# A new order of the pieces, block 1 normalized with ScalarE's negated mean, and two weight loads cut differently

## Chip, cores and metric

The kernel runs on one NeuronCore of a Trainium2 chip. The metric is the device time of one execution in microseconds (us). Below, PE is TensorE, DVE is VectorE, ACT is ScalarE, POOL is GpSimd, and SP is the engine that issues most of the transfers (DMAs).

## The reference

The input is normalized per row. Two branches read the result, and both are added to the input: an attention in which every position looks at itself and at seven earlier positions, two apart, with 32 heads of 20 elements, and a feed-forward layer with a GELU.

```python
# S, D, F, H = 2048, 640, 1536, 32
def _A_ref(x, wqkv, wo):
    Dh = D // H
    W, dil = 8, 2
    qkv = (x @ wqkv).reshape(B, S, 3, H, Dh).transpose(2, 0, 3, 1, 4)
    q, k, v = qkv[0], qkv[1], qkv[2]
    idx = jnp.arange(S)[:, None] - (jnp.arange(W) * dil)[None, :]
    mask = idx >= 0
    ...
    logits = jnp.einsum("bhsd,bhswd->bhsw", q, kg) * Dh ** -0.5
    logits = jnp.where(mask[None, None, :, :], logits, -1e9)
    attn = _softmax(logits, axis=-1)
    o = jnp.einsum("bhsw,bhswd->bhsd", attn, vg)
    return o.transpose(0, 2, 1, 3).reshape(B, S, D) @ wo

def _B_ref(x, w1, b1, w2, b2):
    return jnp.einsum("bsf,fd->bsd", _gelu(jnp.einsum("bsd,df->bsf", x, w1) + b1), w2) + b2

xn = _layernorm(x, axis=-1)
return x + _A_ref(xn, A_wqkv, A_wo) + _B_ref(xn, B_w1, B_b1, B_w2, B_b2)
```

## The kernel before

The 2048 rows are cut into four chunks n = 0 to 3 of 512 rows, and each chunk into four blocks of 128 rows. All products on TensorE work on transposed data: features (or heads) lie on the 128 partitions, rows lie along the free dimension.

The kernel is written as 627 small functions with names, the pieces, and a list `ORDER` (L40) of these names. The last lines run the pieces in this order, and each engine executes its instructions in the order in which they were recorded. The waits between engines are put in by the framework, from which instruction writes or reads which part of a tile, and from what was recorded before. So the list sets all queues at once. A name is made of a kind and of numbers, the first of which is the chunk:

- `st`, `su`, `ng`, `sq`, `rs`, `rc`, `xn`: mean, variance, their reciprocal root, and the normalized rows. In chunks 0 and 1 VectorE finds the statistics (`st`, L210); in chunks 2 and 3, and in block 1 of chunk 0, ScalarE does it: sum (`su`, there `sum1`), negated mean (`ng`, there `neg1`), squares (`sq`). `mean1` (L240) turns ScalarE's sum for block 1 into a mean on VectorE. `xn` of chunk 0 is on VectorE (L263), of the others on ScalarE.
- `tp`, `tc`: the transposition, in chunk 0 by TensorE and a copy, in the others by a DMA from SP (L294).
- `ga`, `gb`, `gd`, `ge`, `gc`, `hj`, `hc`: chunk 0's projections to q, k and v in half width, and ScalarE's evictions. `pj` and `pc` are the same for the other chunks: `pj110` is chunk 1, k (0 is q, 1 is k, 2 is v), tile 0. One `pj` is five matmuls of 512 columns into one result bank of the pool `psA`, which has four; `pc` empties it.
- `pad` (L404): ScalarE copies the last 14 columns of the chunk before to the front of a chunk's k or v, since the window looks back 14 positions. `pad11` is the copy for chunk 1's k.
- `qk` (L430): VectorE multiplies a block of q with the eight shifted windows of k; `pa`, `pb` add tiles, `lg` sums over a head's elements with TensorE into the tile `L`.
- `cp`, `mask`, `m`, `mx`, `ex`, `ss`, `ri`, `at`: the softmax, in chunk 0 in two halves a and b. `ri` is a logarithm and an exponential on ScalarE, so it needs another table of ScalarE than the GELU.
- `xe`, `av`, `ac`, `ad`, `ot`: the weights are spread over the partitions by DMA, multiplied with v and summed.
- `f1`, `ge` (`f10_7` is chunk 0, tile 7): the first feed-forward product (five matmuls into a bank of `psA`) and the GELU that empties it.
- `t`, `u`, `ut`, `ud`: second feed-forward product and output projection into two other banks, eviction with bias, turning back by DMA, and a DMA that adds to the output, where `xp` has put x before. The last chunk's `o` pieces make rows directly, and `dh`, `dl`, `dd` add x and store.
- `ldx`, `ld2`, `ldo`: loads of the later x, of the second feed-forward weights and of the output weights, on SP in the order of the list. The first loads stand ahead of the list.

The list before has, around chunk 0's softmax (dots for pieces left out):

```python
hj201 su23 pb04 ... sq22 pj104 pad11 pc103 lg0 ... mx0a mx0b pj120 qk10 ex0a ...
sq21 qk11 ... ss0b ... ss0a ri0b ... qk13 rs2 hc212 ri0a ... rc2 qk12 f10_8 ge0_4 ge0_7
```

Of the kernel before, what the change touches and what calls it, by code (L numbers as in the profile page):

```python
# [11 lines left out]
ALU = mybir.AluOpType  # L12
# [4 lines left out]
S, D, F, H, W, DIL = 2048, 640, 1536, 32, 8, 2  # L17
# [3 lines left out]
KT, FT = D // P, F // P  # L21
# [16 lines left out]
COLS = ((0, 2), (2, 4), (4, 5))  # L38

ORDER = """  # L40
pad01 pad02 st00a st00 sum1 rs00 neg1 xn00a sq1 xn00b tp00a wa tp00b tc00a wb ga tc00b rs01 mean1 gb2 xn01a gb3 xn01b
tp01a st03a tp01b gb4 tc01a tc01b st02a gd gc0 st02 ge st03 rs02 hj101 xn02 rs03 gc4 xn03 gc1 tp02 st13a tp03 st11a
hj100 tc03 st10a st10 tc02 hj102 st13 hc101 hj012 hc100 st12a hj112 st12 hc102 tb hj111 st11 b1 ho rs1 hj110 hc112 rc1
qk00 hc012 pk xn11 hj011 xn10 tc11 hj200 hc111 hc110 tc10 qk01 hj010 hc011 hc200 f10_11 xn13 hc010 tc13 f10_0 xn12
qk03 f10_3 tc12 f10_1 ge0_11 ldx ge0_0 qk02 f10_5 ge0_1 pj110 ge0_5 ld2 pj114 pc110 pa00 su20 pj102 ge0_3 pj100 pc102
pa01 su22 pj112 pc100 su21 f10_2 pb01 pc114 pj103 ge0_2 pc112 xp2 hj201 su23 pb04 ldo pj101 hc201 ng2 sq22 pj104 pad11
pc103 lg0 pj111 cp0b cp0a pc101 mask pj113 m0b xp0 pc104 m0a pc111 xp1 hj211 pc113 mx0a mx0b pj120 qk10 ex0a pj122
pc120 ex0b t040 sq21 qk11 pj124 pc122 hc211 hj210 sq23 t000 sq20 ss0b hj212 hc210 f10_7 ss0a ri0b pc124 pj121 qk13 rs2
hc212 ri0a f10_4 pc121 f10_6 rc2 qk12 f10_8 ge0_4 ge0_7 t001 xn21 f11_1 xn20 tc21 at0b ge0_8 pa11 t041 ge0_6 tc20
pj123 f11_10 xn23 pa10 ge1_1 tc23 f11_9 xn22 ge1_10 f10_9 tc22 at0a pc123 pb11 ge1_9 hj202 xe01 su33 t042 xe03 f11_3  # L50
pad21 xe00 su32 pb14 pj210 ge1_3 xe02 pj203 pc210 su31 lg1 hc202 t002 su30 av01 pj204 ng3 ge0_9 pj214 sq32 pc204 pj211
av00 pc203 ac01 pad12 pc214 pj200 sq30 f11_0 pc200 pc211 av02 ac00 f11_5 sq31 cp1a f10_10 cp1b ge1_0 pj213 av03 ge0_10
ge1_5 pj201 pc213 sq33 t003 pj221 m1 t043 mx1 rs3 pj224 pc221 ac03 ex1 pj202 pc201 rc3 ss1 xn31 pj220 pc202 tc31 ac02
f11_6 pc224 ri1 pj223 at1 ad01 xe11 pj222 pc223 xe12 xe13 pj212 ad00 pc222 xn32 f12_3 xe10 pc220 ot00 xn33 f11_2 ot01
tc32 av11 t004 t044 u00 tc33 t010 u04 av12 t011 ut00 xn30 t012 t030 tc30 t013 av13 t014 ud00 t031 u01 ac11 t032 t033
ac12 t020 t034 ge1_6 av10 ge2_3 t021 pc212 t022 f12_4 ac13 ac10 t023 ge2_4 t024 u03 ut01 xb ad11 f12_6 ot11 pj302 qk22
f11_8 pc302 ge1_2 f11_7 pj303 qk23 ge1_7 ge1_8 pj311 ge2_6 pc303 pj300 pa21 t140 pc300 pj310 f11_11 ad10 pj314 ge1_11
ot10 pc311 f11_4 pc310 qk20 pj301 ge1_4 pc314 pj313 u02 pc301 ut02 t130 qk21 pc313 f13_6 pad31 pad22 ut03 t141 ut04
ud01 pj304 pa20 pj312 ud02 t142 pc312 f12_9 pb21 pc304 ud03 ge3_6 f13_4 t143 pb24 f12_2 f13_1 ge2_2 ge2_9 lg2 f12_10
qk31 cp2a ge3_4 t131 cp2b t132 t133 t134 m2 qk30 f13_0 f13_2 ge3_0 ge2_10 t144 u13 mx2 ge3_2 pj321 qk32 u14 ge3_1  # L60
pj322 t100 pa30 t110 ex2 t101 f13_5 qk33 t102 ge3_5 f13_10 pad32 pc321 pc322 t103 t104 ss2 t111 pa31 ri2 f12_0 u10
f13_3 ut10 at2 f13_8 pb31 xe20 t120 xe22 ge3_8 t112 xe21 ge2_0 t113 ge3_3 pb34 f12_8 xe23 t114 lg3 u11 f12_11 cp3a
av20 ut11 ud10 cp3b f13_9 ge2_11 ge3_10 f13_7 ge2_8 m3 ge3_9 f12_5 ac20 ge3_7 mx3 t121 av21 f12_1 ex3 t122 o300 ss3
t123 ac21 ge2_1 f13_11 av23 t124 ri3 o301 u12 f12_7 at3 av22 pj323 xe31 ge2_5 ut12 ud11 ud04 ge2_7 pj324 t200 t201
ac22 xe30 t230 ut13 pj320 ac23 o302 pc320 ad21 pc323 t202 pc324 xe33 t231 ge3_11 ut14 ad20 t232 o310 ot21 t233 ot20
t203 o311 av31 t204 t234 u20 ut20 av30 t210 u23 ud12 t211 xe32 t212 t213 t214 ac30 t220 u21 ac31 t221 t222 t223 ad30
t224 av33 t240 u22 ud13 ud20 ut21 ud14 t241 t242 t243 ac33 o330 o331 t244 o303 u24 ud21 ut22 ot30 o320 av32 o304 ud22
ut23 ut24 o321 ud23 o312 ac32 o313 dh0 dl0 o332 ad31 o322 dd0 o314 ud24 ot31 o323 dl1 o324 dh1 dd1 o333 dl2 o334 dh2
dd2 ohi dl3 dlo dh3 dhi
""".split()  # L70


# [1 line left out]
def kernel(  # L74
# [16 lines left out]
    nc = tc.nc  # L91
# [23 lines left out]
    wqkv = [wts.tile([P, KT, D], BF16, name=f"w{s}_sb") for s in "qkv"]  # L115
# [5 lines left out]
    wqkv_v = A_wqkv.rearrange("(t p) n -> p t n", p=P)  # L121
    w1_v = B_w1.rearrange("(t p) n -> p t n", p=P)

    def load_x(b0, b1):
        nc.sync.dma_start(x_sb[:, b0:b1, :], x_nb[:, b0:b1, :])

    def load_w(s):
        nc.sync.dma_start(wqkv[s][:], wqkv_v[:, :, s * D : (s + 1) * D])
# [3 lines left out]
    nc.scalar.dma_start(x_sb[:, 1, :], x_nb[:, 1, :])  # L132
    nc.scalar.dma_start(b_rt[0:FT, :], B_b1.rearrange("(t p) -> t p", p=P))
    nc.scalar.dma_start(b_rt[FT : FT + KT, :], B_b2.rearrange("(t p) -> t p", p=P))
    load_w(0)
    load_x(2, BPC)
    load_w(1)
    load_x(BPC, 2 * BPC)
# [9 lines left out]

    def do_ld2():
        w2_v = B_w2.rearrange("(t p) n -> p t n", p=P)  # L150
        for c in range(4):
            ts = slice(c * FT // 4, (c + 1) * FT // 4)
            nc.sync.dma_start(w2_sb[:, ts, :], w2_v[:, ts, :])

    def do_ldo():
# [11 lines left out]
    def table(name):  # L167
# [6 lines left out]
    mask = consts.tile([H, W, MW], BF16, name="mask")  # L174
    nc.gpsimd.memset(mask[:], 0.0)
    nc.gpsimd.affine_select(
        out=mask[:],
# [16 lines left out]
    mv = consts.tile([P, NCH * BPC, nc.vector.BN_AGGR_DIM], F32, name="mv")  # L194
# [3 lines left out]
    acc = consts.tile([P, NCH * BPC], F32, name="acc")  # L198
    neg = consts.tile([P, NCH * BPC], F32, name="neg")
# [17 lines left out]
    def xn_tile(n, bl):  # L217
        return get(("xn", n, bl), lambda: lnp.tile([P, D], BF16, tag="xn", name="xn"))

    def col(tile_, n, bl):  # L220
        i = n * BPC + bl
        return tile_[:, i : i + 1]
# [14 lines left out]
            accum_out=mv[:, n * BPC + bl, 1:2],  # L237
        )

    def do_mean1():  # L240
        nc.vector.tensor_scalar(
            out=mv[:, 1, 0:1], in0=col(acc, 0, 1), scalar1=1.0 / D, scalar2=None, op0=ALU.mult
        )

    def do_rs(n, b0, b1):
        sl = slice(n * BPC + b0, n * BPC + b1)
        summed = n in ACT_STATS or (n, b0) == (0, 1)
        table(LOG_SET)
        nc.scalar.activation(
            logv[:, sl], mv[:, sl, 1], ACT.Ln, bias=eps_t[:], scale=1.0 / D if summed else 1.0  # L250
        )
        nc.scalar.activation(rstd[:, sl], logv[:, sl], ACT.Exp, scale=-0.5)
# [10 lines left out]
    def do_xn(n, bl, a=0, b=KT):  # L263
        i, cs = n * BPC + bl, slice(a * P, b * P)
        xn = xn_tile(n, bl)
        if n:
            nc.scalar.activation(xn[:], x_sb[:, i, :], ACT.Identity, bias=col(nmr, n, bl), scale=col(rstd, n, bl))
            return
        nc.vector.tensor_scalar(
            out=xn[:, cs],  # L270
            in0=x_sb[:, i, cs],
            scalar1=mv[:, i, 0:1],
            scalar2=rstd[:, i : i + 1],
            op0=ALU.subtract,
            op1=ALU.mult,
        )

# [444 lines left out]
    def piece(name, fn, *args):  # L722
        assert name not in pieces
        pieces[name] = lambda: fn(*args)

    for name in "tb b1 mean1 ho ldx ld2 ldo ohi mask pk xb".split():
        piece(name, locals()[f"do_{name}"])
    for u, a, b, eng in (("a", 0, 2, "ve"), ("b", 2, KT, "se")):
        for bl in range(2):
            piece(f"xn0{bl}{u}", do_xn, 0, bl, a, b)  # L730
            piece(f"tp0{bl}{u}", do_tp, 0, bl, a, b, True)
        piece(f"tc00{u}", do_tc, 0, 0, a, b, "ve")
        piece(f"tc01{u}", do_tc, 0, 1, a, b, eng)
    for bl in range(BPC):
        if bl != 1:
            piece(f"st0{bl}a", do_st, 0, bl, 0)
            piece(f"st0{bl}", do_st, 0, bl, 1)
        piece(f"rs0{bl}", do_rs, 0, bl, bl + 1)
        if bl > 1:
            piece(f"xn0{bl}", do_xn, 0, bl)  # L740
            piece(f"tp0{bl}", do_tp, 0, bl, 0, KT)
            piece(f"tc0{bl}", do_tc, 0, bl, 0, KT, "se")
# [119 lines left out]
```

## Time and profile before

| | |
|---|---|
| median of 3 runs | 206.21 us (205.78 to 206.46) |
| the profiled execution | 205.85 us, its span 203.8 us |
| TensorE busy | 199.1 us, 98% of the span |
| VectorE busy | 186.3 us, 91% |
| ScalarE busy | 128.7 us, 63% |
| DMA | 27.31 MB, mean 134 GB/s |
| GELU evictions `hT<-hps` on ScalarE | 36, 686 ns each |
| evictions `kT<-pps` on ScalarE | 15, 594 ns each |
| ScalarE's table loads | 14, 1283 ns each |
| products `prod<-qT,kT` on VectorE | 16, 2820 ns each |

The span goes from the first to the last instruction that was profiled; the time of an execution has some 2 us around it. An engine's busy time is the union of its instructions. Lines of the view by time give the start in us, the time until the last of the group ended, engine, line of the program, operation, what is written and what is read, sizes, and how many instructions stand in the group; in brackets the idle time of the engine before it and who ended it.

### The profile page before, as it was taken

Reading aid. Unit: us, or ns where it says so; the run is one execution under the profiler, and the core shown is the slowest. Engines: PE = TensorE matmul, PEld = TensorE weight load, DVE = VectorE, ACT = ScalarE, POOL = GpSimd, SP = SyncE. Lnnn points to the kernel's source line nnn. Section 1 sums busy time; section 2 is a strip of 40 time slices with the busy share of each in tenths; the row PEclk is TensorE's granted clock in tenths of the full one; section 3 lists DMA queues with packets and bytes.
Section 4 is the critical chain, followed back from the end, with each engine's and each line's share of the span. In section 5 each row is a group of like instructions: output and inputs, shape, how many; then the busy total and the mean of one; then the engine's idle time right before and its main releaser. Section 6 shows DMA issues by size and latency. Waiting matters only on the chain.

```text
span 203.8 us, 2855 instructions
## 1 busy us (share of the span) xinstructions
PE 199.1 (98%) x1082; PEld 105.7 (52%) x1100; DVE 186.3 (91%) x161; ACT 128.7 (63%) x237; POOL 29.4 (14%) x34
## 2 busy tenths in 40 slices
PE   8999999999999999999999999999999999999994
PEld 3999456564454455444454443444434454444552
DVE  2899999699998999999999997999978999998972
ACT  5679988799899997647264635398669923221000
POOL 2000000000000400004420040000202704046210
PEclk9999999999999999999999999999999999999999
DMA  6996499910246681779896190000496799897851
GB/s 213 388 397 197 120 328 341 400 72 3 64 86 184 112 148 32 164 147 117 144 152 71 37 92 0 3 0 0 92 186 123 126 169 129 97 106 88 77 90 64
DMA packets 38430, 27.31 MB, mean 134 GB/s; under 512 B 25106, under 2 KB 34578, under 8 KB 38418
## 3 DMA queue, kind: packets, MB, share of 16 engines
q1 hardware_dynamic: 28016, 20.39, 37.4%
q0 software_dynamic: 10080, 6.56, 27.2%
q10 hardware_dynamic: 322, 0.20, 0.3%
q8 instruction: 8, 0.13, 0.3%
q14 instruction: 4, 0.03, 0.0%
HBM read 10.49 MB, written 4.59 MB: 74 GB/s over the span
## 4 chain that ended last, share of the span: by engine, by line
PE 96%; ACT 1%; issue 1%; DVE 0%
PE T L701 27%; PE hps L619 25%; PE pps L338 23%; PE gps L382 7%; PE lo L657 5%; PE idle L448 2%; PE both L657 2%; PE gps L351 2%; PE hi L657 1%; PE L L485 1%; ACT x_sb L704 1%; PE tp L284 1%; ACT wq_sb L635 1%; ACT hT L635 0%; DVE prod L669 0%
## 5 line engine op out<-in xcount | busy, mean ns | idle before, releaser
L619 PE MATMUL hps<-xnT,w_sb 128*128 128x512 bf16 x231 | 55.8, 379 | 0.4
L435 DVE TENSOR_TENSOR prod<-qT,kT 128x5120 bf16<-128x5120 bf16 x16 | 44.6, 2820 | 1.2 <-PE L L485 1.0
L701 PE MATMUL T<-hT,w_sb 128*128 128x512 bf16 x179 | 44.0, 379 | 0.1
L619 PEld LDWEIGHTS <-w_sb 128*128 128x128 bf16 x240 | 23.3, 98 | 28.0 <-issue 1.0
L713 POOL DMA_DIRECT2D out_dram<-x_sb x15 | 19.7, 1430 | 84.0 <-DMA x_sb<-x_sb 63.0
L635 ACT ACTIVATE hT<-hps,bT 128x512 bf16<-128x512 f32 x36 | 23.5, 686 | 9.4 <-PE hps L619 9.1
L701 PEld LDWEIGHTS <-w_sb 128*128 128x128 bf16 x180 | 17.4, 98 | 20.5 <-issue 0.4
L704 ACT ACTIVATE x_sb<-T,bT 128x512 bf16<-128x512 f32 x15 | 10.3, 687 | 21.8 <-PE T L701 14.8
L589 DVE TENSOR_TENSOR prod<-vT,ax 128x5120 bf16<-128x5120 bf16 x8 | 22.3, 2821 | 1.8 <-PE L L485 1.8
L589 DVE TENSOR_TENSOR prod<-vT,x_sb 128x5120 bf16<-128x5120 bf16 x8 | 22.3, 2820 | 0.1
L600 POOL DMA_DIRECT2D prod<-prod x6 | 7.8, 1300 | 80.4 <-DVE prod L589 80.4
L170 ACT ACT_TABLE_LOAD x14 | 18.0, 1283 | 1.0 <-PEq L846 0.7
L476 DVE TENSOR_TENSOR prod<-prod 128x4096 bf16<-128x4096 bf16 x8 | 18.3, 2290 | 0.2
L338 PE MATMUL pps<-xnT,wq_sb 128*128 128x512 bf16 x74 | 18.3, 379 | 0.1
L701 PE MATMUL T<-oT,wo 128*128 128x512 bf16 x73 | 18.2, 379 | 0.1
L470 DVE TENSOR_TENSOR prod<-prod 128x4096 bf16<-128x4096 bf16 x8 | 18.1, 2286 | 0.1
L338 PE MATMUL pps<-xnT,wk_sb 128*128 128x512 bf16 x75 | 18.2, 379 | 0.0
L338 PE MATMUL pps<-xnT,wv_sb 128*128 128x512 bf16 x71 | 17.8, 379 | 0.2
L602 DVE TENSOR_TENSOR prod<-prod 128x2560 bf16<-128x2560 bf16 x10 | 14.7, 1488 | 0.1
L338 PEld LDWEIGHTS <-wk_sb 128*128 128x128 bf16 x75 | 8.7, 118 | 7.7 <-issue 0.4
L338 PEld LDWEIGHTS <-wv_sb 128*128 128x128 bf16 x75 | 8.8, 117 | 7.4
L338 PEld LDWEIGHTS <-wq_sb 128*128 128x128 bf16 x75 | 8.8, 117 | 7.3
(96 smaller groups left out, 241.5 us busy)
## 6 DMA issues: line engine op xcount, KB each, us to landing
prod<-prod POOLq DMA_DIRECT2D x6, 640.0 KB, 7.0
ax<-attn SPq DMA_DIRECT2D x8, 256.0 KB, 4.3
x_sb<-attn SPq DMA_DIRECT2D x8, 256.0 KB, 4.8
w_sb<-in_B_w_dram SPq DMA_DIRECT2D x2, 960.0 KB, 11.3
w_sb<-in_B_w_dram SPq DMA_DIRECT2D x4, 480.0 KB, 8.2
out_dram<-x_sb SPq DMA_DIRECT2D x3, 640.0 KB, 9.5
out_dram<-x_sb POOLq DMA_DIRECT2D x15, 128.0 KB, 5.1
x_sb<-in_A_x_dram SPq DMA_DIRECT2D x2, 640.0 KB, 6.9
```

Of the source, the lines that this page charges most:

```text
L170: nc.scalar.preload_act_table_set(name)
L338: nc.tensor.matmul(ps[:], lhsT=wqkv_p[which][:, ti, to, :], rhs=xnT[:, ti, :], start=(ti == 0), stop=(ti == KT - 1),)
L435: nc.vector.tensor_tensor(out=prod[:, j], in0=q[:, :, at].unsqueeze(1).to_broadcast([P, W, KT, P]), in1=window(k, at), op=ALU.mult,)
L470: nc.vector.tensor_tensor(out=low, in0=low, in1=high, op=ALU.add)
L476: nc.vector.tensor_tensor(out=first, in0=first, in1=rows[:, :, t * P : (t + 1) * P], op=ALU.add)
L589: nc.vector.tensor_tensor(out=prod[:, j], in0=window(qkv_tile(n, 2), slice(j * P, (j + 1) * P)), in1=ax_view(n)[:, j, :, :].unsqueeze(2).t ...
L602: nc.vector.tensor_tensor(out=low, in0=low, in1=high, op=ALU.add)
L619: nc.tensor.matmul(ps[:], lhsT=w1_sb[:, ti, ft * P : (ft + 1) * P], rhs=tiles["xnT", n][:, ti, :], start=(ti == 0), stop=(ti == KT - 1),)
L635: nc.scalar.activation(hT, tiles["hps", n, ft][:], ACT.Gelu_apprx_tanh, bias=bT[:, ft : ft + 1], scale=1.0)
L657: nc.tensor.matmul(out_ps(bl, hi), lhsT=lhs, rhs=rhs[:, CH:D] if hi else rhs[:, 0:CH], start=pc == 0 and k == 0, stop=pc == 4 and k == len ...
L701: nc.tensor.matmul(ps[:], lhsT=lhs, rhs=rhs, start=pc == 0 and k == 0, stop=pc == 4 and k == len(srcs) - 1)
L713: nc.gpsimd.dma_start(dst, src, accum_op=ALU.add)
```

## The change

Four things are changed.

- The list of pieces is in another order. It holds the same pieces but `mean1`.
- `mean1` is gone. Block 1 of chunk 0 is normalized by adding ScalarE's negated mean instead of subtracting a mean.
- q's weights are loaded by two DMAs (two and three of the five slices of 128 input features), not by one.
- The second feed-forward weights are loaded by three DMAs of four tiles, not by four of three.

```diff
-    load_w(0)
+    for a, b in ((0, 2), (2, KT)):
+        nc.sync.dma_start(wqkv[0][:, a:b, :], wqkv_v[:, a:b, 0:D])
     load_x(2, BPC)
...
     def do_ld2():
         w2_v = B_w2.rearrange("(t p) n -> p t n", p=P)
-        for c in range(4):
-            ts = slice(c * FT // 4, (c + 1) * FT // 4)
+        for c in range(3):
+            ts = slice(c * FT // 3, (c + 1) * FT // 3)
             nc.sync.dma_start(w2_sb[:, ts, :], w2_v[:, ts, :])
...
-    def do_mean1():
-        nc.vector.tensor_scalar(
-            out=mv[:, 1, 0:1], in0=col(acc, 0, 1), scalar1=1.0 / D, scalar2=None, op0=ALU.mult
-        )
...
             in0=x_sb[:, i, cs],
-            scalar1=mv[:, i, 0:1],
+            scalar1=neg[:, 1:2] if bl == 1 else mv[:, i, 0:1],
             scalar2=rstd[:, i : i + 1],
-            op0=ALU.subtract,
+            op0=ALU.add if bl == 1 else ALU.subtract,
             op1=ALU.mult,
```

The new list, from the first pieces, and around chunk 0's softmax:

```python
pad01 pad02 st00a st00 sum1 ho rs00 neg1 xn00a sq1 xn00b tp00a wa tp00b wb tc00a tc00b rs01 ga xn01a gb2 xn01b tp01a
gb3 st02a tb tp01b tc01a gb4 st02 tc01b gd gc0 st03a ge rs02 st03 hj101 b1 xn02 rs03 gc4 xn03 gc1 tp02 st12a tp03
...
qk02 f10_1 tc12 ge0_0 f10_5 ldx qk03 f10_11 ge0_5 f10_3 ge0_11 ge0_2 pj101 ge0_3 pa00 pj112 pc101 ge0_1 pj104 pc112
xp2 pa01 su20 pj110 xp0 pc104 ld2 su22 pj102 pc110 pb01 pj100 su21 hj201 su23 pc102 pb04 pj103 ng2 pc100 hc201 pj114
sq22 lg0 pc114 ldo pj111 cp0b cp0a sq21 mask pj113 m0b pc103 m0a pj124 pc111 mx0a pc113 mx0b t000 qk11 pj120 ex0b
hj202 ex0a hj210 pc120 sq23 ss0a hj211 pc124 ss0b sq20 pj122 qk13 hc202 rs2 f10_7 pad11 hc211 pc122 t040 ri0b f10_8
ri0a rc2 qk12 hc210 f10_4 f11_1 ge0_7 xn21 qk10 f11_3 ge0_4 tc21 xn20 pj121 ge1_3 tc20 t041 ge1_1 pa11 f11_9 ge0_8
...
```

On the queues of SP and POOL the same kinds of DMAs stand in another order. `xp2` and `xp0` now come ahead of the second feed-forward weights, `xp1` behind the four expansions `xe00` to `xe03`; three of the DMA additions (`ac`) precede the first addition to the output, where two did.

## The prediction

> **What bounds the kernel now.** I read the page's totals, the slices, the chain that ended last, TensorE's waits, and then the order of time on TensorE, ScalarE and VectorE where the two orders differ.
>
> ```profile
> span 203.8 us, 2855 instructions
> PE 199.1 (98%) x1082; PEld 105.7 (52%) x1100; DVE 186.3 (91%) x161; ACT 128.7 (63%) x237; POOL 29.4 (14%) x34
> ...
> PEclk9999999999999999999999999999999999999999
> ...
> PE 96%; ACT 1%; issue 1%; DVE 0%
> ```
>
> TensorE is busy for 98% of the span at full clock, and the chain lies 96% on it. TensorE's list of waits has one line, 0.8 us before the first warm-up matmul. From about 9 us to 200.8 us the matmuls stand almost end to end: 25 matmuls of 512 columns take 5.39 us start to start, 0.2157 us each. So the change can win only what little is not dense. A piece that comes late for TensorE is paid in full, as nothing behind it has slack to absorb it. Hence I looked where the new order makes TensorE wait.
>
> Its result banks (`psA`, four) are emptied by ScalarE in queue order. Around chunk 0's softmax the view by time shows before:
>
> ```profile
> 35.81 0.62 PE L485 MATMUL L<-prod,head_of 128*32 128x512 bf16 x8
> 44.62 0.81 PE L701 MATMUL T<-hT,w_sb 128*128 128x512 bf16 x3
> 45.81 1.24 PE L619 MATMUL hps<-xnT,w_sb 128*128 128x512 bf16 x5
> 47.97 3.40 PE L619 MATMUL hps<-xnT,w_sb 128*128 128x512 bf16 x14
> 51.21 0.81 PE L701 MATMUL T<-hT,w_sb 128*128 128x512 bf16 x3
> ```
> ```profile
> 35.31 0.23 ACT L409 COPY kT<-kT 128x70 bf16<-128x70 bf16 x1
> 37.20 0.58 ACT L525 CAST e<-L 128x512 bf16<-128x512 f32 x1 [1.18 <-DVE e L525]
> 39.76 1.28 ACT L170 ACT_TABLE_LOAD   x1
> 46.63 0.26 ACT L557 ACTIVATE ax<-ax 128x64 f32<-128x64 f32 x1
> 49.27 1.28 ACT L170 ACT_TABLE_LOAD   x1
> 50.57 1.26 ACT L635 ACTIVATE hT<-hps,bT 128x512 bf16<-128x512 f32 x2
> ```
> ```profile
> 36.48 0.69 DVE L525 CAST e<-L 128x512 bf16<-128x512 f32 x1 [0.86 <-PE L L485]
> 40.12 5.56 DVE L435 TENSOR_TENSOR prod<-qT,kT 128x5120 bf16<-128x5120 bf16 x2
> 45.59 0.42 DVE L532 TENSOR_TENSOR ax<-e 128x256 f32<-128x256 bf16 x1
> 46.51 0.42 DVE L532 TENSOR_TENSOR ax<-e 128x256 f32<-128x256 bf16 x1
> 47.44 2.82 DVE L435 TENSOR_TENSOR prod<-qT,kT 128x5120 bf16<-128x5120 bf16 x1
> ```
>
> The reader should see three things. The small copy `pad11` (35.31, L409) starts with no idle time before it, five microseconds ahead of the first product of chunk 1 (40.12). ScalarE is full from 37.2 to 54 us. TensorE meets no gap over that stretch.
>
> **The change part by part.**
>
> *pad11 behind qk11 and qk13.* In the new order `pad11` stands after both products. It writes the first 14 columns of each tile of chunk 1's `kT`; the products read other columns of the same tiles, in interleaved strips. The program built from the changed file has a wait before this copy for the VectorE count that `qk13` reaches. The old one has none. Everything behind `pad11` on ScalarE waits too: `hc211`, `pc122`, both reciprocals, `hc210`, the GELU table, `ge0_7`. TensorE needs the banks that these free.
>
> I lay out both queues from the start of `lg0`, 35.78 (35.81 before; the order ahead of it has the same matmul work). VectorE up to `qk11` is as before, 40.12-35.81 = 4.31 later: 40.09. `qk11` takes 2.74 to the next start (two took 45.59-40.12 = 5.47): 42.83. The two sums now follow at once, 0.92 each (46.51-45.59): 44.67. `qk13` 2.82: done 47.49. Hand-over from VectorE to ScalarE takes 0.03 in this trace (median of six starts): `pad11` starts 47.52.
>
> ScalarE: `cp0a` 37.17, then 0.48 to `sq21`, 0.82 for it, three evictions at 0.477 with 0.17 more before the table load, table 1.29, two exponentials 0.53 each, `pc120` 0.47, `sq23` 0.81, so `pc124` starts 43.71 and is done 44.29. After it come `sq20` 0.81, `hc202` 0.25 and `rs2` 0.5: ScalarE would reach `pad11` at about 45.8. It stands idle 1.7 us there.
>
> TensorE from 35.78: `lg0` 0.55, two k pieces 2.16, `pj124` 1.08, `t000` 0.65, `pj120` 1.08, 25 matmuls of 256 columns 2.72: ready for `pj122` at 44.02. Its four waits, with 0.04 from ScalarE's end to TensorE's start:
> - `pj122` needs `pc124`: 44.33, a stall of 0.3. Then `pj122`, `f10_7` and `t040` (1.08+1.08+0.65) end at 47.14.
> - `f10_8` needs `hc211`: 47.52+0.14 (pad to next, 35.31 to 35.45) = 47.66, +0.59 = 48.25; 48.29, a stall of 1.15.
> - `f11_3`, three pieces later at 51.52, needs `ge0_7`: 47.66 + two evictions 0.95 + two reciprocals 0.90 + `hc210` 0.58 + table 1.29 + GELU 0.69 = 52.07; 52.11, a stall of 0.6.
> - `pj121`, at 53.19, needs `ge0_4`, which stands behind `xn21`: 51.38+0.58+0.81+0.69 = 53.46; 53.50, a stall of 0.3.
>
> Then `f11_9` at about 55.2 finds a bank free at 54.9, and ScalarE is caught up. Sum 2.35. Taken alone, `pj122`'s 0.3 does not come from `pad11`. Without the wait, `f10_8` and `f11_3` find their banks (1.7 earlier) and `pj121` about 0.3 late. So 0.6 belongs to the order and 1.75 to the wait. VectorE loses 0.3, since `qk12` waits for `pad11`; TensorE is then over 2 us later, which more than pays for it.
>
> *Block 1 without `mean1`.* One VectorE instruction less:
>
> ```profile
> 6.48 0.14 DVE L241 TENSOR_SCALAR mv<-acc 128x1 f32<-128x1 f32 x1
> 6.71 0.64 DVE L269 TENSOR_SCALAR xn<-x_sb,mv,rstd 128x256 bf16<-128x256 bf16 x2
> ```
>
> The normalization waits for `rs01` (done 6.50) and could begin up to 0.17 earlier. TensorE has one gap there: two starts 0.154 apart at 8.05 where 0.056 is usual. Gain 0 to 0.1; I take 0.05. `ho` moves ahead of `xn00a` (0.28 of VectorE work); VectorE is idle 0.66 there, so nothing. Without that cover it would delay the first transposes by 0.28.
>
> *q's weights in two parts.* They landed at 5.88 before and were first needed at 6.17. Two of five slices land earlier, the rest must be there when the first ten matmuls are done. One more issue on SP, 0.42, sits ahead of x's blocks 2 and 3, k's weights and all later loads. Blocks 2 and 3 landed 6.99 and were read 7.26; k's weights landed 9.02 and were needed 9.60. Queued bytes, not issues, set these landings (299 GB/s in the first 10 us), so I take 0. At worst 0.42-0.27 = 0.15.
>
> *Second feed-forward weights in three, after `xp2` and `xp0`.* One issue less (0.5). Ahead of the first part now lie two writes of 0.66 MB; at the 400 GB/s that the stretch 36 to 40 us moved, that is 3.3 us, and 31.4 becomes about 35. `t000` reads it at 39.6, so the cover is 4.6 us. `xp1` moves behind the first expansions; x's first rows are overwritten only near 81 us. Both 0.
>
> *The rest of the order* moves evictions by places in their queues. Elsewhere I found each bank emptied at least 0.15 before its reuse. Before had about 0.2 of such gaps itself (two starts 0.40 apart at 57.7), which the new order may lose.
>
> Sum: +2.35 - 0.05 - 0.1 = +2.2. The profiled execution took 205.85 (span 203.8 and 2.05 around it): 208.05. The runs shown have median 206.21, 0.36 above it, so the sum could read 208.4. Since single terms might shrink by overlap, I stay with 208.0.
>
> **The clock.** The granted clock is full in all slices, yet 128-column matmuls start 0.107 apart up to 6.6 us and 0.056 after.
> The Trainium skill ("TensorE: Matmul & The Clock Gate", section "A second HAM failure mode: psum-queue depth-cycling") says that TensorE idling briefly between groups, as banks cycle, can drop its clock again; no run here shows it, as before has no such idling.
>
> **The rivals.**
> 1. *The stall is hidden or absent.* The strips do not truly overlap, so the wait might cost little if `qk13` were earlier, or ScalarE later. For: `pad11` is 0.23 us of work. Against: VectorE is 91% busy and `qk13` cannot start before both sums. Then 0.0 to 0.6 remain: about 206.2.
> 2. *Faster.* The head decides: block 1 earlier, q's weights earlier, and the gaps at 8.05 (0.1), 57.7 (0.2) and around `lg0` (0.2) close, from the point where no bank in 44 to 54 us is late. 205.85-0.5 = 205.35. Against: these are all the gaps there are.
> 3. *The idling takes the clock down.* Price from this trace: the slow stretch at the start lasted from 0.78 to 6.65; half of 5.87 is 2.9 lost. 208.0+2.9 = 210.9. Against: four stalls of which the longest is 1.15. That page of the Trainium skill would have it happen.
> 4. *A transfer comes late too* (x's blocks, or the transposes behind the three moved writes): a further 0.5 to 1, some 208.8.
>
> **How the numbers follow.** Forecast 0.76 (207.3 to 208.7 by itself), rival 1 0.11, rival 2 0.03, rival 3 0.03, rival 4 0.07. About 0.3%, 0.6 us, can be told from no change; against 206.21, faster means below 205.6 and slower above 206.8. Rival 2 gives faster 0.03; rival 1 gives same 0.10 and, with the rest, slower 0.87. The range 206.7 to 209.0 leaves out most of rivals 1 to 3, under 2 in 10.
>
> **What would show it.** After: ScalarE's `kT<-kT` copy starts near 47.5, behind 1.7 us idle released by VectorE's product; TensorE's starts show gaps near 44, 47 to 48 (about 1.1), 52 and 53, and nowhere else over 0.3; the GELU table load comes near 50.1. It is wrong if the copy does not wait, if the gaps sum to under 1, or if gaps appear after 60 us.

## The result, and the profile after

| | before | after |
|---|---|---|
| median | 206.06 us (5 runs, 205.78 to 206.46) | 208.92 us (5 runs, 208.13 to 209.28) |
| profiled execution | 205.85 us, span 203.8 us | 208.92 us, span 206.9 us |
| TensorE busy | 199.1 us | 200.0 us |
| VectorE / ScalarE busy | 186.3 / 128.7 us | 185.8 / 129.0 us |

The ratio is 1.0135, with a 95% interval from 1.0112 to 1.0158: the change costs 2.9 us. In a few executions of the kernels below the granted clock is lower and the time some 2% longer (212.27 us in one of e2_whole_q), and the ratios leave most of these out. The work is the same to within a microsecond on each engine, so the time went into waits. The page of after, from its totals, its slices and its chain:

```profile
span 206.9 us, 2869 instructions
PE 200.0 (97%) x1100; PEld 104.9 (51%) x1100; DVE 185.8 (90%) x160; ACT 129.0 (62%) x237; POOL 29.4 (14%) x34
...
PEclk9999999999999999999999999999999999999999
...
PE 78%; ACT 7%; DVE 7%; DMA 5%; issue 1%
```

The granted clock is full in every slice. The chain, 96% TensorE before, now leaves TensorE for a fifth of the span: there are places where TensorE waits for ScalarE, VectorE and a DMA. TensorE's list of waits in after (line, what it waited for, us in total, times, longest) names them:

```profile
PE hps L615 <- ACT vT L393: 1.0, 1, 1.0
PE hps L615 <- ACT hT L631: 0.8, 2, 0.4
PE idle L444 <- PEq L842: 0.8, 1, 0.8
PE tp L280 <- DVE xn L265: 0.7, 1, 0.7
PE gps L347 <- DVE xn L265: 0.5, 1, 0.5
PE gps L347 <- DVE xnT L285: 0.2, 1, 0.2
```

Before, only the third of these lines was there. The others fall into two places, but for one of the two waits for `hT`, at 24.9, which e3_both below has too at no loss that can be told. The first place is chunk 0's softmax. TensorE, ScalarE and VectorE there, in the view by time of after (start, time until the group's last end, and in brackets the idle time before and who ended it):

```profile
36.91 0.61 PE L481 MATMUL L<-prod,head_of 128*32 128x512 bf16 x8
...
46.52 1.24 PE L615 MATMUL hps<-xnT,w_sb 128*128 128x512 bf16 x5
47.60 0.81 PE L697 MATMUL T<-hT,w_sb 128*128 128x512 bf16 x3
49.44 3.40 PE L615 MATMUL hps<-xnT,w_sb 128*128 128x512 bf16 x15 [1.03 <-ACT vT L393]
53.27 1.24 PE L615 MATMUL hps<-xnT,w_sb 128*128 128x512 bf16 x5 [0.44 <-ACT hT L631]
```
```profile
48.65 0.25 ACT L405 COPY kT<-kT 128x70 bf16<-128x70 bf16 x1 [1.75 <-DVE prod L431]
48.80 0.58 ACT L393 CAST vT<-gps 128x512 bf16<-128x512 f32 x1
...
51.24 1.28 ACT L171 ACT_TABLE_LOAD   x1
52.53 0.69 ACT L631 ACTIVATE hT<-hps,bT 128x512 bf16<-128x512 f32 x1
```
```profile
45.80 2.82 DVE L431 TENSOR_TENSOR prod<-qT,kT 128x5120 bf16<-128x5120 bf16 x1
48.93 5.56 DVE L431 TENSOR_TENSOR prod<-qT,kT 128x5120 bf16<-128x5120 bf16 x2 [0.24 <-ACT kT L405]
```

Read from the copy outwards. The copy `pad11` (48.65, L405) stands behind 1.75 us of idle ScalarE. VectorE's product `qk13`, 45.80 to 48.62, ended that idle time. The eviction of `hc211` starts right behind the copy at 48.80, and TensorE's `f10_8`, which needs the bank, starts at 49.44 after 1.03 us. Start to start, four TensorE gaps above the matmuls' usual pitch lie between 44 and 55 us: 0.21 before `pj122`, 1.19 before `f10_8`, 0.61 before `f11_3`, 0.31 before `pj121`; together 2.32 us.

The second place is the head. `lg0`, the first line of the TensorE fence, starts at 36.91, and before at 35.81: after arrives 1.1 us late at the stretch that the prediction laid out. The head of after on TensorE, from the same view, and then VectorE's first statistics of a block loaded by the later DMA, in after and in before:

```profile
6.07 0.72 PE L347 MATMUL gps<-xnT,wq_sb 128*128 128x128 bf16 x10
7.26 0.47 PE L347 MATMUL gps<-xnT,wq_sb 128*128 128x128 bf16 x5 [0.48 <-DVE xn L265]
...
8.16 0.44 PE L347 MATMUL gps<-xnT,wq_sb 128*128 128x128 bf16 x5
8.81 1.39 PE L347 MATMUL gps<-xnT,wq_sb 128*128 128x128 bf16 x22 [0.21 <-DVE xnT L285]
```
```profile
8.08 0.49 DVE L214 BATCH_NORM_STATS2 stats<-x_sb 128x6 f32<-128x320 bf16 x1 [0.84 <-DMA x_sb<-in_A_x_dram]
7.26 0.49 DVE L213 BATCH_NORM_STATS2 stats<-x_sb 128x6 f32<-128x320 bf16 x1
```

The first ten matmuls of q (`ga`) use the two slices that land first. The eleventh needs the second part and starts 0.7 us after the tenth; it waits for that load's semaphore. The line names VectorE's `xn` as the releaser, but these matmuls do not read it: they read `xnT` of block 0 and q's weights. `xn` of block 1 only happened to end at 7.24. What the matmul waited for, the second part of q's weights, landed at 7.22; a second execution of the same kernel, below, has the DMA's name in this place. Further on, x's blocks 2 and 3 landed at 8.05 (6.99 before), and VectorE waits 0.84 us for them, which it did not before (`st02a`, 7.26 there, no idle time).

1.1 + 2.3 = 3.4 us. Of this some 0.4 comes back by the end: before had a gap of 0.19 near 58 us that after has not, and what follows the last matmul takes 2.8 us in after's span, 3.0 in before's. That leaves 3.0 of the 3.1 us between the two spans.

### The profile page after: what moved, and what is told of

Its sections match the earlier page's. It is cut to its first block, busy times and chain, and to the rows that moved or that the text cites. A ratio compares the mean times of both kernels' runs of the same rounds, so it can differ in the third digit from the quotient of the medians.

```text
span 206.9 us, 2869 instructions
## 1 busy us (share of the span) xinstructions
PE 200.0 (97%) x1100; PEld 104.9 (51%) x1100; DVE 185.8 (90%) x160; ACT 129.0 (62%) x237; POOL 29.4 (14%) x34
## 4 chain that ended last, share of the span: by engine, by line
PE 78%; ACT 7%; DVE 7%; DMA 5%; issue 1%
PE T L697 26%; PE pps L334 21%; PE hps L615 20%; DMA x_sb<-in_A_x_dram 5%; PE lo L653 5%; DVE prod L431 3%; PE both L653 2%; ACT xn L263 2%; DVE stats L214 2%; PE hi L653 1%; ACT L171 1%; PE L L481 1%; ACT hT L631 1%; DVE ax L530 1%; PE gps L378 1%; ACT vT L393 1%
## 5 line engine op out<-in xcount | busy, mean ns | idle before, releaser
L615 PE MATMUL hps<-xnT,w_sb 128*128 128x512 bf16 x240 | 56.4, 379 | 1.8 <-ACT vT L393 1.0
L697 PE MATMUL T<-hT,w_sb 128*128 128x512 bf16 x180 | 44.6, 379 | 0.0
L709 POOL DMA_DIRECT2D out_dram<-x_sb x15 | 20.8, 1614 | 67.5 <-DMA x_sb<-x_sb 66.2
L596 POOL DMA_DIRECT2D prod<-prod x6 | 7.3, 1208 | 101.3 <-DVE prod L585 101.3
L334 PE MATMUL pps<-xnT,wv_sb 128*128 128x512 bf16 x75 | 18.3, 379 | 0.2
L398 ACT CAST qT<-pps 128x512 bf16<-128x512 f32 x15 | 8.6, 582 | 7.2 <-PE pps L334 7.2
```

Source lines behind the costliest of these rows:

```text
L334: nc.tensor.matmul(ps[:], lhsT=wqkv_p[which][:, ti, to, :], rhs=xnT[:, ti, :], start=(ti == 0), stop=(ti == KT - 1),)
L615: nc.tensor.matmul(ps[:], lhsT=w1_sb[:, ti, ft * P : (ft + 1) * P], rhs=tiles["xnT", n][:, ti, :], start=(ti == 0), stop=(ti == KT - 1),)
L697: nc.tensor.matmul(ps[:], lhsT=lhs, rhs=rhs, start=pc == 0 and k == 0, stop=pc == 4 and k == len(srcs) - 1)
L709: nc.gpsimd.dma_start(dst, src, accum_op=ALU.add)
```

## The experiments

Two theories at first: the copy's wait is all that matters (the prediction's), or part of the loss comes from q's weights in two parts. After and three kernels make a square of the two edits; the three were timed in five rounds together with the kernel before (206.09 us there). After that, why the cut costs anything was asked, and whether the copy's place alone, in the old order, does what the new order showed.

**pad11 early (e1_pad_early): after, with the copy ahead of the products.**

```diff
-... ng2 pc100 hc201 pj114 sq22 lg0 ... qk11 ... qk13 hc202 rs2 f10_7 pad11 hc211 ...
+... ng2 pc100 hc201 pj114 sq22 pad11 lg0 ... qk11 ... qk13 hc202 rs2 f10_7 hc211 ...
```

> The changed kernel with pad11 moved back ahead of lg0, nothing else. Theory (the wait of pad11 for qk13 costs 1.75 of the 2.9 us): ScalarE is not idle before the copy, the gap of 1.19 us before f10_8 and that of 0.61 before f11_3 are gone, that of 0.3 before pj121 and of 0.2 before pj122 stay; 208.9 - 1.8 = 207.1 us. Rival (the banks are late for another reason, as ScalarE is full there): the gaps stay or move, 208.3 to 208.9 us. The gaps of the first 10 us (0.65 and 0.38) stay under both.

Measured: 206.76 us, ratio to before 1.0023 (1.0000 to 1.0045). Two of TensorE's waits in this kernel, and its view by time where the stalls were:

```profile
PE gps L347 <- DMA wq_sb<-in_A_wqkv_dram: 0.7, 1, 0.7
PE hps L615 <- ACT hT L631: 0.3, 1, 0.3
```
```profile
47.56 0.81 PE L697 MATMUL T<-hT,w_sb 128*128 128x512 bf16 x3
48.21 4.48 PE L615 MATMUL hps<-xnT,w_sb 128*128 128x512 bf16 x19
52.62 1.24 PE L334 MATMUL pps<-xnT,wv_sb 128*128 128x512 bf16 x5
```

Behind `pj122` no gap over 0.1 is left up to 56 us. The wait for `hT` that is left is the one near 24.9. One name moved in the list takes 208.92 - 206.76 = 2.2 us away. The head's waits stay, and now one of them names q's weights as what TensorE waited for.

**q's weights whole (e2_whole_q, and profiled again as e7_whole_q_look): after, with one load.**

```diff
-    for a, b in ((0, 2), (2, KT)):
-        nc.sync.dma_start(wqkv[0][:, a:b, :], wqkv_v[:, a:b, 0:D])
+    load_w(0)
```

> The changed kernel with q's weights in one DMA again, nothing else. Theory (the cut of q's load makes the later part, and all loads behind it, land about 1.1 us later): q's weights land at about 5.9, x's blocks 2 and 3 at 7.0, the gaps of 0.65 and 0.38 us in TensorE's first 10 us are gone; 208.9 - 1.0 = 207.9 us. Rival (the landings were late in that one execution, or the order's head is what waits): 208.7 to 208.9 us, gaps stay.

Measured: 207.95 us, ratio 1.0075 (1.0049 to 1.0101). The profile of this kernel is a second one:

> The changed kernel with q's weights in one DMA, a second profile: q's weights land near 5.9, TensorE's gaps of 0.65 and 0.38 us in the first 10 us are gone, those of 1.2 and 0.6 us around 50 us stay; about 207.9 us.

That execution took 207.49 us. TensorE's waits in it, but for the one before the first matmul:

```profile
PE hps L614 <- ACT vT L392: 1.0, 1, 1.0
PE hps L614 <- ACT hT L630: 0.4, 1, 0.4
```

Now the head's waits are gone and the softmax's stay (gaps of 1.20, 0.60 and 0.31 start to start). q's weights landed at 5.89 and x's blocks 2 and 3 at 6.72. The cut is worth 208.92 - 207.95 = 1.0 us with the copy's wait in place.

**Both undone (e3_both).**

> The changed kernel with both undone: pad11 ahead of lg0 and q's weights in one DMA. If the two causes are separate and are all there is, their savings add: 208.9 - 1.8 - 1.0 = 206.1 us, the time of before. If one hides behind the other or a third is at work (the rest of the order), 206.8 us or more.

Measured: 205.94 us, ratio 0.9978 (0.9956 to 1.0001). The square, medians:

| us | copy late | copy early |
|---|---|---|
| q's weights cut | 208.92 | 206.76 |
| q's weights whole | 207.95 | 205.94 |

The copy's wait costs 2.2 or 2.0 us, the cut 1.0 or 0.8, and they add up. What is left of the change, the rest of the order, block 1 without `mean1` and the second feed-forward weights in three, is 205.94 against 206.09: nothing that can be told.

**The cut alone, in the kernel before (e4_before_split).**

```diff
-    load_w(0)
+    for a, b in ((0, 2), (2, KT)):
+        nc.sync.dma_start(wqkv[0][:, a:b, :], wqkv_v[:, a:b, 0:D])
```

> The kernel before with q's weights loaded in two parts, nothing else. Theory (the cut itself makes loads late): the second part lands near 7.2 and TensorE waits in the first 10 us; 206.1 + 1.0 = 207.1 us. Rival (the cut is harmless, the new order's head is at fault): 206.1 us, same as before.

Measured: 207.12 us, ratio 1.0051 (1.0025 to 1.0076); its quickest execution of 12, 206.65, is above before's median. The cut costs 1.0 us in the old order, without anything else of the change. TensorE's and VectorE's idle times in the head of this kernel, from the view by time:

```profile
8.07 1.56 PE L352 MATMUL gps<-xnT,wq_sb 128*128 128x128 bf16 x25 [0.23 <-DVE xnT L290]
9.60 0.63 PE L383 MATMUL gps<-xnT,wk_sb 128*128 128x256 bf16 x4
...
18.75 1.25 PE L383 MATMUL gps<-xnT,wq_sb 128*128 128x256 bf16 x10 [0.17 <-ACT kT L398]
```
```profile
7.34 0.49 DVE L214 BATCH_NORM_STATS2 stats<-x_sb 128x6 f32<-128x320 bf16 x1 [0.38 <-DMA x_sb<-in_A_x_dram]
...
11.24 1.67 DVE L214 BATCH_NORM_STATS2 stats<-x_sb 128x6 f32<-128x320 bf16 x4 [0.54 <-DMA x_sb<-in_A_x_dram]
```

Here the loss takes another way to TensorE. k's projection starts at 9.60, just as before, so TensorE's own gaps in the head are not what it pays for. But x's later blocks come late (4 to 7 at about 11.2, not 10.7), VectorE's statistics of chunk 1 end 0.5 us later (15.14 + 0.21 against 14.65 + 0.21), ScalarE waits for them before it goes on with evictions, and TensorE meets this as a late bank: `gps` at 18.75, not 18.38.

By the last matmul the kernel is 0.7 us behind the one before. Another 0.4 of the 1.1 us between the two spans lies after it (3.4 us to the end, not 3.0), and that part comes from the number of the DMAs, not from a landing. The DMAs that SP and ScalarE issue take eight semaphores in turn: 72 DMAs before, 73 here. So the last store takes the eighth semaphore before, and the first here. At the end of the program SP waits for all eight, one after the other, the first one first. The last store lands 2.1 us after the start of the last matmul in both. Before, SP has passed the other seven by then; here it still stands at the first (one wait of 1.6 us, where before has two, together 1.2), and the other seven take it 0.43 us more. e5, e6 and e9 below, with 73 DMAs too, have the same 3.4 us; e10 and e11 with 72 have 3.0, as before. After has 72 as well (one more for q's weights, one fewer for the second feed-forward weights), and with q's weights whole 71, at 2.8 us both. So in the new order the end is the same with and without the cut, and its 0.8 to 1.0 us lie elsewhere, in the head; in the old order 0.4 of its 1.0 is this.

**Why does a cut cost anything? The bias rows (e5_split_bias_late): the kernel above, with the two small loads of bias rows issued later.**

```diff
-    nc.scalar.dma_start(b_rt[0:FT, :], B_b1.rearrange("(t p) -> t p", p=P))
-    nc.scalar.dma_start(b_rt[FT : FT + KT, :], B_b2.rearrange("(t p) -> t p", p=P))
...
     load_x(BPC, 2 * BPC)
+    nc.sync.dma_start(b_rt[0:FT, :], B_b1.rearrange("(t p) -> t p", p=P))
+    nc.sync.dma_start(b_rt[FT : FT + KT, :], B_b2.rearrange("(t p) -> t p", p=P))
```

> The kernel before with q's weights in two parts, and the two small bias loads issued by SP behind x's blocks 4 to 7 instead of by ScalarE at the start. Theory A (the rows of the bias loads fall between the two parts on a few of the 16 DMA engines and hold those up): the second part lands near 5.9 on all engines, 206.1 us. Theory B (one more load at the start costs by itself, whatever else is queued): the last landing stays at 6.5 or later, 207.1 us as with the cut alone.

Measured: 207.57 us, ratio 1.0056 (1.0032 to 1.0081), q's second part at 6.59, x's blocks 2 and 3 at 7.76. The idea that the bias rows' packets come between the two parts falls.

**Any early load cut (e6_split_k): before, with k's weights in two and three slices.**

```diff
-    load_w(1)
+    for a, b in ((0, 2), (2, KT)):
+        nc.sync.dma_start(wqkv[1][:, a:b, :], wqkv_v[:, a:b, D : 2 * D])
```

> The kernel before with k's weights in two parts, q's in one. Theory B (any further load among the first ones costs about 1 us of landing): k's second part lands near 10 instead of 9.0, x's blocks 4 to 7 near 11.7 instead of 10.7, and TensorE waits: 206.6 to 207.1 us. Theory A (only what is queued beside the bias loads): landings as before, 206.1 us.

Measured: 206.66 us, ratio 1.0014 (0.9976 to 1.0053): no difference that can be told. k's second part landed at 9.09 (whole: 9.02) and x's blocks 4 to 7 at 10.75 (10.67). The landings decide where the time does not: one more DMA with the same bytes, issued while others are still queued, delays nothing here. The last matmul starts 0.03 us later than before, and the 0.45 us between the two spans is the end of the program, as in e4. So the late landings are not the cost of an issue; that they belong to the place in the head where little is queued is an inference.

**The change once more (e8_after_look).**

> The changed kernel as it is, a second profile: if the cut load is late by rule, its second part lands near 7 again and the gaps in the first 10 us are there again; about 208.9 us. If it was chance, it lands near 6 and the time is near 207.9 us.

Measured: 209.31 us in this one execution, with q's second part at 7.82. TensorE's three longest waits that bear on this:

```profile
PE gps L347 <- DMA wq_sb<-in_A_wqkv_dram: 1.1, 1, 1.1
PE hps L615 <- ACT vT L393: 1.0, 1, 1.0
PE hps L615 <- ACT hT L631: 0.8, 2, 0.4
```

The two lines on `vT` and `hT` are those of the first execution, to the digit. The head is not: TensorE waits 1.1 us for q's weights where it had waited 0.5. The wait at the copy is the same each time; the late landing differs from one execution to the next, and after's five runs spread over 1.15 us, before's over 0.68.

**The cut elsewhere (e9_split_four_one): before, with parts of four and one slices.**

```diff
-    load_w(0)
+    for a, b in ((0, 4), (4, KT)):
+        nc.sync.dma_start(wqkv[0][:, a:b, :], wqkv_v[:, a:b, 0:D])
```

> The kernel before, with q's weights cut into parts of four and one slices instead of one load. Cut into two and three slices it took 207.12 us (1.0051), and the second part landed at 6.48 us instead of 5.88. Theory 'the first part runs out before the second is ready' (two slices are about 0.9 us of packets on each DMA engine, four are 1.8): the last landing of q's weights stays near 5.9 us, x's blocks 2 and 3 near 7.0, no gap of TensorE in the first 10 us over 0.25, time 206.1. Rival, 'any cut of q's load costs this much, wherever it lies': second part at 6.5 or later, x's blocks at 7.3 or later, time 207.1.

Measured: 206.71 us, ratio 1.0005 (0.9971 to 1.0039). The last part landed at 6.14, as the first theory wants, and TensorE has no wait in the head. x's blocks 2 and 3, at 7.24, lie between the two expectations, and so does the median, 0.6 above the 206.12 of the kernel before that was timed with it, while the ratio's interval holds 1. Of the 0.8 us between the two profiled spans 0.4 is the end of the program, as in e4, so 0.4 at most is left for the landings. e6 pays the same end. Against e6 and e9, with medians of 206.66 and 206.71, the cut into two and three slices (207.12 in e4, 207.57 in e5) is 0.4 to 0.9 us slower. This leans to "where the cut lies matters" and does not settle it.

**A control (e10_qk_permuted): before, with chunk 1's products in another order at the same places.**

```diff
-... pj120 qk10 ex0a ... sq21 qk11 pj124 ... pj121 qk13 rs2 ... rc2 qk12 f10_8 ...
+... pj120 qk13 ex0a ... sq21 qk11 pj124 ... pj121 qk12 rs2 ... rc2 qk10 f10_8 ...
```

> A control: the kernel before with the four products of chunk 1's k in the order qk13, qk11, qk12, qk10 at the same four places of the list, pad11 in its old place ahead of all. No wait is added, and the sums that read them come later than all four. Both theories: as before, 206.1 us (206.0 to 206.6), no gap of TensorE between 36 and 60 us over 0.2.

Measured: 206.32 us, ratio 1.0006 (0.9980 to 1.0031): as before. The execution that was profiled took 206.97, at the upper end of its 12, and shows why. The TensorE wait it had:

```profile
PE gps L351 <- DVE xn L269: 1.1, 1, 1.1
```

q's weights, one load here, had landed in 15 of 16 parts by 6.11; the last came at 7.23, and x's blocks, k's and v's weights each had one part about 1.1 us behind the others. `xn`, which the line names, is no operand here either (the kernel before had started these matmuls at 6.17, ahead of `xn` at 6.71). So a late part is seen without the cut too, here and in the execution of e2_whole_q that took 212.27 us (8.43).

**The copy late, in the old order (e11_pad_late): the control, with `pad11` behind two products.**

```diff
-... ng2 sq22 pj104 pad11 pc103 lg0 ... sq21 qk11 pj124 ...
+... ng2 sq22 pj104 pc103 lg0 ... sq21 qk11 pad11 pj124 ...
```

> The control with pad11 moved right behind qk11, the second product in its list; the order is otherwise the kernel before's, and nothing else of the change is in it. Theory of the wait (ScalarE's copy waits for both products, and the evictions behind it come late): the copy starts near 45.7 us behind some 2.3 us of idle ScalarE, TensorE has gaps of about 1.5 and 1.0 us between 43 and 50 us, time about 208.5 us (206.1 + 2.4). Rival (the new order's evictions are what starves TensorE, the copy's place is harmless without them): the copy starts within 0.5 us of the work ahead of it, no such gaps, 206.1 us.

Measured: 208.24 us, ratio 1.0094 (1.0060 to 1.0128). Nothing of the change is in this kernel but the place of one small copy. ScalarE and TensorE by time:

```profile
45.75 0.25 ACT L409 COPY kT<-kT 128x70 bf16<-128x70 bf16 x1 [2.26 <-DVE prod L435]
```
```profile
44.60 0.81 PE L701 MATMUL T<-hT,w_sb 128*128 128x512 bf16 x3
46.54 0.70 PE L382 MATMUL gps<-xnT,wv_sb 128*128 128x256 bf16 x5 [1.12 <-ACT vT L402]
47.08 1.24 PE L619 MATMUL hps<-xnT,w_sb 128*128 128x512 bf16 x5
49.27 1.24 PE L338 MATMUL pps<-xnT,wv_sb 128*128 128x512 bf16 x5 [0.94 <-ACT vT L397]
```

The copy starts at 45.75 (expected 45.7) behind 2.26 us (2.3), and the two gaps are 1.29 and 1.11 start to start (1.5 and 1.0). The rival, by which the new order's evictions starve TensorE, falls. The median is 1.9 above the control's and 2.1 above before's; the gaps add to 2.4.

**The order alone (e12_order_alone): the new list with the copy early, and all other edits undone.**

```diff
-... ng2 pc100 hc201 pj114 sq22 lg0 ... qk13 hc202 rs2 f10_7 pad11 hc211 ...
+... ng2 pc100 hc201 pj114 sq22 pad11 lg0 ... qk13 hc202 rs2 f10_7 hc211 ...
...
-    for a, b in ((0, 2), (2, KT)):
-        nc.sync.dma_start(wqkv[0][:, a:b, :], wqkv_v[:, a:b, 0:D])
+    load_w(0)
...
-        for c in range(3):
-            ts = slice(c * FT // 3, (c + 1) * FT // 3)
+        for c in range(4):
+            ts = slice(c * FT // 4, (c + 1) * FT // 4)
...
-            scalar1=neg[:, 1:2] if bl == 1 else mv[:, i, 0:1],
+            scalar1=mv[:, i, 0:1],
```

> The new list with pad11 put ahead of the products, mean1 back on VectorE, q's weights in one load and the second feed-forward weights in four: of the change, the order alone, without the copy's wait. Theory (mean1 and the cut of the second feed-forward weights are worth nothing): 205.9 to 206.1 us, as the kernel that has these two edits as well (205.94). Rival (they win something that the order loses): over 206.4 us. My prediction's split, 0.6 of the stalls from the order even without the wait, gives 206.06 + 0.6 = 206.7 us.

Measured: 206.16 us, ratio 0.9999 (0.9971 to 1.0028). `lg0` starts at 35.87, as before (35.81), so with q's weights whole the new order's head loses nothing. The order without the wait is worth nothing, and `mean1` and the cut of the second feed-forward weights, which set this kernel apart from e3_both (205.94), are worth nothing that can be told either. No kernel here beats the one before by more than can be told from no change.

## Why the prediction was right, and what it left out

**The wait.** Right in mechanism, place and size. `pad11` waits for `qk13` and stands behind 1.75 us of idle ScalarE (1.7 foreseen); the GELU's table load comes at 51.24, which is 1.1 after the 50.1 of the text, as is everything from `lg0` on, since that started 1.1 late. The four gaps:

| before | foreseen | in after | in e12 (same order, no wait) |
|---|---|---|---|
| `pj122` | 0.3 | 0.21 | 0.21 |
| `f10_8` | 1.15 | 1.19 | none |
| `f11_3` | 0.6 | 0.61 | none |
| `pj121` | 0.3 | 0.31 | 0.10 |
| sum | 2.35 | 2.32 | 0.31 |

The split into 1.75 for the wait and 0.6 for the order was off: `pj121` waits 0.1, not 0.3, once the copy is early. The wait has 2.0 of the 2.3 (the sums of the last two columns differ by that), which agrees with the 2.0 and 2.2 of the square.

**q's weights in two parts.** This is the term that failed: "so I take 0. At worst 0.15". It measured 0.8 to 1.0 (the square). The step behind it was "Queued bytes, not issues, set these landings". I counted one more issue and no more bytes. The runs show that issues are indeed not the matter for the landings (k's cut moved none), but also that equal bytes did not land at equal times. In the kernels with q cut into two and three slices the last part came at 6.48 to 7.82 in all five profiles, against 5.87 to 6.15 in six of the eight with one load. The prediction had written down that x's blocks 2 and 3 landed 0.27 before they were read; and the second part of q's weights is needed when ten matmuls are done, at about 6.6 in after. In four of the five profiles the second part came too late for TensorE (waits of 0.2 to 1.25 us start to start), and in all five x's blocks, at 7.31 to 8.64, came behind the 7.26 at which they were read before. Why equal bytes land later in two loads stays open.

**Block 1 without `mean1`**, 0.05, and the gaps that before had, 0.1: neither can be told from nothing (e3_both: -0.15 for these, the rest of the order and the next edit). **The second feed-forward weights in three**: 0, as taken.

**The sum.** Foreseen +2.2, measured +2.9 by the medians and +3.1 by the two profiled executions; the difference is mostly q's weights. Of the 0.9 us between 208.0 and 208.92, 0.2 is the base (205.85 of one execution, where the median is 206.06) and 0.7 is what the sum left out. The measured time lies inside the stated range, which holds rival 4 as well, by 0.08 us; two of the five executions (209.03 and 209.28) lie above it. That the total still came out within it, with one term taken as 0, is in part luck. Rival 4, "a transfer comes late too", with "a further 0.5 to 1, some 208.8", came true on top of the forecast, at a place other than the two it named first: x's blocks were late, but behind q's own weights. The text also said that no gap over 0.3 would be seen outside the softmax. After has four (at the start of the matmul ahead of the gap): 0.64 at 6.57 and 0.38 at 8.38 from the landings; 0.84 at 4.50, where the warm-up matmuls ended early at full clock and the first transposes waited for `xn`; and 0.5 at 24.2, where a bank waited for a GELU, which e3_both has too at no loss.

**The other rivals.** The first (stall hidden) falls with the 1.75 us of idle ScalarE. The second (the head gains) falls in its sign: the head lost 1.1 us. The third priced a drop of the clock at 2.9 us. After's granted clock is full in all 40 slices, and behind the gap of 1.19 us the matmuls of 512 columns start 0.216 us apart again, as ahead of it. The Trainium skill ("TensorE: Matmul & The Clock Gate", section "A second HAM failure mode: psum-queue depth-cycling") tells of a kernel in which such idling between groups, frequent enough, took the clock down. It doesn't say how frequent; four gaps of 0.2 to 1.2 us did not do it here.

## What to carry to other kernels

A small copy in an in-order queue costs what it waits for, and what it waits for is decided by which instructions were recorded before it, not by the bytes it touches: before moving one behind another engine's long instructions, see whether it shares a tile with them and what stands behind it. When a wait shows a cover of 0.3 us at a landing in the head, price the landing's spread, and not only the extra issue. One more DMA can also cost at the end of the program, where the semaphores are waited for in order: 0.4 us in four kernels here. A stall laid out from the durations of the old profile, queue by queue, came out within 0.1 us for each gap; the term put at 0 was the one that was wrong.

## What the runs showed of the hardware

**The same bytes in two loads land later.** Landing times below are read from the sixteen updates that end a transfer; the last one counts.

| kernel | q's weights | x's blocks 2 and 3 | GB/s from 4.0 to 5.4 us |
|---|---|---|---|
| one load: before, e7, e3, e12, e11, e6 | 5.88, 5.89, 5.87, 5.98, 6.12, 6.15 | 6.99, 6.72, 7.48, 6.81, 6.95, 7.19 | 388, 392, 389, 389, 385, 385 |
| one load: e10, e2's execution of 212.27 us | 7.23, 8.43 | 8.12, 9.26 | 373, 357 |
| four and one slices, e9 | 6.14 | 7.24 | 375 |
| two and three slices: e4, e5, after, e1, e8 | 6.48, 6.59, 7.22, 7.28, 7.82 | 7.31, 7.76, 8.05, 8.10, 8.64 | 315, 311, 313, 293, 327 |

In the cut kernels most of the sixteen land near 5.4 to 5.9, as in the others, and the rest later, the last of them 0.3 to 2 us behind the usual time; what is queued behind is late by about as much. An explanation that fits is that the first part is done before the second part's packets are ready, and the engines fall out of step. The first part is about 0.9 us of packets on each DMA engine, an estimate from x's blocks 2 and 3 of before: they are as many bytes, and most of them landed 0.9 us behind most of q's weights. The last column speaks for it: right behind the first part's landing (most of it by 4.5 us) the DMAs of the five cut kernels moved 293 to 327 GB/s, those of the others 357 to 392. e9, whose first part is twice as long, leans that way too. It isn't shown: the runs do not tell what kept the second part's packets back, and e10 and e2 have a late part with no cut at all.

**The clock comes up at different times, and the start of the softmax doesn't show it.** The granted clock is full from 3.5 us in e4, 3.7 in after, 4.3 in e8, 4.4 in e6, 4.8 in e11, 5.1 in e10, 6.2 in e9, 6.7 in before and 6.8 in e5, although the first warm-up matmul starts at 0.78 in all of them. Before, e6 and e11 have the same head, with q's weights in one load. e6 and e11 start k's projection 0.2 us sooner (9.39 and 9.36, not 9.60), and all three start `lg0` at 35.8: two microseconds more at full clock show as nothing by then. The Trainium skill (the same page, section "What's actually happening") has a window of 3.4 us that runs freely, and a transition that varies by 0.5 us each way. The spread of 3.2 us here fits a free window and not the 0.5.
